# Moving a row gather, the weight casts of the first and last group, and the seam's small copies in a fused attention and mixer block

## The chip, the cores and the metric

The kernel runs as one launch on one NeuronCore of a Trainium2 chip. The metric is the device time of one execution in microseconds. The core has five engines with a queue each, and every queue runs in order: TensorE (PE; its weight loads are listed as PEld), VectorE (DVE), ScalarE (ACT), GpSimd (POOL) and SyncE (SP). SP and POOL issue the DMAs; POOL's are used where a transfer adds to what lies at its target.

## The reference

Everything is fp32, with x of 2048 rows (tokens) by 576 columns:

```python
xn  = layernorm(x)
out = x + A(xn) + B(xn)
# A: 32 heads of 18 columns; a token attends to itself and to 7 earlier tokens, 2 rows apart
q, k, v = split(xn @ wqkv);  A = softmax(q.k/sqrt(18), 8 taps) . v  @ wo
# B: spatial shift, then channel mixing
h  = gelu(layernorm(xn) @ w1)          # 576 x 576
hs = shift4(h, +1, -1, +2, -2) @ w2    # a quarter of the columns each, 576 x 576
x1 = xn + hs
B  = x1 + gelu(layernorm(x1) @ w3) @ w4   # 576 x 4608 and 4608 x 576
```

## The kernel before, in words

**Products in three parts.** A number is split into a high part that TensorE's fast fp32 format holds and the low rest. A product is then high by high, high by low and low by high. "Casting" an operand is always the same pair: ACT writes the high part (a copy or activation into the fp32r tile), and DVE subtracts it from the raw value and writes the low part. A raw operand comes by DMA, so the pair waits for its landing, and as ACT's queue runs in order, a cast that waits holds up whatever ACT has behind it: above all the copies that empty TensorE's PSUM banks.

**Stages, in order of time.** (1) q, k, v products (line 215 and 314), written to memory. (2) First mixing stage, lines 507 to 529: for each of 4 blocks `b` of 512 tokens, four tiles of W1's columns and one tile of remainders (`mix_rem`, line 478, PE line 482), in a fixed order; the block's input `xt` is read back by `get` (line 172) and cast by `split_x` (line 177). `mix_rem` also sends eight small transfers `v<-u` on SP. In the block `b == 1` SP also gathers tail rows of w3 from memory to memory into `w3t` (line 521), in two transfers, to be used much later. (3) Second mixing stage, line 628: 16 tiles `t` of 128 tokens (PE line 215), each with statistics on DVE and POOL; `n_turn` (582) normalises and transposes on ACT and DVE, and SP writes the turned blocks `xn` and reads them back (`get_n`). (4) Six plain pairs of W3's columns, line 1006: `up` (828, PE line 832) and `down` (859, PE line 868). (5) The rest of W3, 24 groups `q` (line 1192), twelve for each half `sb` of the tokens. Group 12 (`NWP`) is the first of the second half: around it lies the seam, where all seven token operands are loaded and cast anew (`get_op` 911, `split_op` 921). (6) The last eight `down` tiles (line 1391) and the product with Wo (1412 on).

**A group of stage 5.** It has seven products of half size (P1 to P7, Strassen's scheme, PE line 1127) and eight `down` tiles of the group before (D0 to D7, PE line 868). Their order on PE is written out in `ORDER`:

```
    ORDER = "P1 D0 P2 P6 D1 P5 D2 P7 D3 P4 D4 P3 D5 D6 D7"
    ORDERS = {0: "P1 P2 D0 P6 P5 P7 D1 D2 P4 D3 P3",
              NWP - 1: "P1 D0 P2 P6 P5 P7 D1 P4 P3 D2 D3 D4 D5 D6 D7",
              NWP: "D0 D1 P1 D2 P2 P6 D3 P5 P7 D4 P4 P3 D5 D6 D7"}
```

Behind each step the code issues that step's own work (emptying the bank: line 873 or 876 on ACT, 879 on DVE; seeding the next bank: 849; `keep`, ACT line 1133, saves a partial sum before PE adds to it; `z_add`, DVE line 1137; the gelus, ACT lines 814 to 821, and their low parts, DVE line 826), and then what `at(step, ...)` has planned there:

- `split_a(q)` casts W3's columns for the next group's products P1, P2 and P4 (A11, A12, A22). Step 0 is ACT line 967, step 1 is ACT line 969 on the tail rows and a POOL transfer that adds `w3t` (line 980), step 2 is DVE line 973. It waits for the pair's raw rows (`load_pair`, SP lines 951 and 954).
- `combine(q)` makes the sums of quarters in place (four DVE operations, line 962), and `split_s(q)` casts these for P3, P5, P6 and P7 (ACT 967 and 969, POOL 989, DVE 973).
- `split_w4` casts W4's rows (ACT 573, DVE 576), `split_wo(k)` one of Wo's five row blocks (ACT 200, DVE 201), which `load_wo` (line 1163) fetches at the start of the last group. In the last groups `o_turn`, `load_o` and `put_o` also turn and move the attention's output.

`split_op` works on one token operand: part 0 is ACT line 927 and DVE line 601 on the 256 main rows; part 1 is ACT line 932 (32 rows of the tail into a spare tile `r`), ACT line 933, and DVE line 601 on the tail.

**Attention** is a generator (`attention`, line 684) that fills DVE's time from stage 4 to group 18. For each of 8 groups of heads it multiplies q with k (line 746) and reduces (749) for 8 taps `w`, in singles and in doubles of two taps, and then weighs v (722, 726). `bg` lets it run for as long as a count of planned DVE time (`spent`) leaves over.

## Time and profile before

| | |
|---|---|
| time, median of 3 runs | 1281.77 us (1280.82 to 1283.99) |
| the profiled execution: its own time, its span | 1281.23 us, 1279.4 us |
| busy: PE, PEld, DVE, ACT, POOL | 98%, 90%, 70%, 57%, 20% of the span |
| TensorE's granted clock | 1.0 throughout |
| mean DMA rate | 174 GB/s |
| PE by stage 4's and 5's lines | L868 486.4 us, L1127 300.5 us, L832 157.0 us |

A row of a timeline has the start, the duration, the engine, the line, the operation and its tiles, and how often it is repeated; in brackets stands the idle time of the engine before it and what ended that. A row of waits has who waited and for whom, then the sum in us, how often, and the longest. `PE ps L868` is PE's instruction on tile `ps` at line 868; `SPq` is SP's queue, whose rows are DMA issues and not transfers.

### The profile page before, as it was taken

Reading aid. Unit: us, or ns where it says so; the run is one execution under the profiler, and the core shown is the slowest. Engines: PE = TensorE matmul, PEld = TensorE weight load, DVE = VectorE, ACT = ScalarE, POOL = GpSimd, SP = SyncE. Lnnn points to the kernel's source line nnn. Section 1 sums busy time; section 2 is a strip of 40 time slices with the busy share of each in tenths; the row PEclk is TensorE's granted clock in tenths of the full one; section 3 lists DMA queues with packets and bytes.
Section 4 is the critical chain, followed back from the end, with each engine's and each line's share of the span. In section 5 each row is a group of like instructions: output and inputs, shape, how many; then the busy total and the mean of one; then the engine's idle time right before and its main releaser. Section 6 shows DMA issues by size and latency. Waiting matters only on the chain.

```text
span 1279.4 us, 19983 instructions
## 1 busy us (share of the span) xinstructions
PE 1259.2 (98%) x7510; PEld 1154.4 (90%) x7510; DVE 897.7 (70%) x1196; ACT 727.3 (57%) x1162; POOL 252.8 (20%) x366
## 2 busy tenths in 40 slices
PE   8999999999999999999999999999999999999999
PEld 8999998799889998999889998998889999888898
DVE  6455534677648999998659998989798983554341
ACT  3332125525645545455777777776867776676630
POOL 2011100011122121212123232232121222222200
PEclk9999999999999999999999999999999999999999
DMA  7646784326887987769669988888958668899982
GB/s 207 154 122 140 166 173 144 103 87 196 209 237 166 223 149 164 150 141 242 120 143 205 199 173 214 201 174 223 259 92 184 124 110 192 178 211 216 256 247 84
DMA packets 203801, 223.25 MB, mean 174 GB/s; under 512 B 79528, under 2 KB 139528, under 8 KB 203576
## 3 DMA queue, kind: packets, MB, share of 16 engines
q1 hardware_dynamic: 170952, 155.18, 42.9%
q0 software_dynamic: 32752, 66.80, 32.1%
q8 instruction: 59, 0.97, 0.3%
q14 instruction: 38, 0.31, 0.1%
HBM read 124.47 MB, written 107.87 MB: 182 GB/s over the span
## 4 chain that ended last, share of the span: by engine, by line
PE 58%; DMA 6%; issue 3%; ACT 2%; DVE 1%; SPq 1%; POOL 0%; ACTq 0%; POOLq 0%; DVEq 0%
PE ps L868 27%; PE cc L1127 17%; PE p L832 9%; PE ps L215 4%; DMA w3st<-in_B_w_dram 2%; DMA xt<-td1T 1%; DMA v<-qkvd 1%; DMA td0T<-xn 1%; DMA x1n<-xd 1%; DVE L L749 0%; DMA x1n<-xn 0%; DMA w3s<-w3st 0%; DVE po L746 0%; SPq L1163 0%; PE p L1436 0%
## 5 line engine op out<-in xcount | busy, mean ns | idle before, releaser
L868 PEld LDWEIGHTS ps<-w,c 128*128 128x128 f32 x3456 | 475.3, 188 | 21.4 <-ACT Y L873 4.1
L868 PE MATMUL ps<-w,c 128*128 128x288 f32 x3456 | 486.4, 294 | 5.3 <-ACT Y L873 2.8
L874 POOL DMA_DIRECT2D yd<-Y x154 | 139.5, 909 | 389.8 <-ACT Y L873 317.4
L826 DVE TENSOR_TENSOR c<-Y,c 128x512 fp32r<-128x512 f32 x144 | 98.7, 687 | 89.5 <-ACT Y L815 87.0
L873 ACT COPY Y<-ps 128x576 f32<-128x576 f32 x154 | 98.0, 637 | 75.3 <-PE ps L868 66.3
L215 PE MATMUL ps<-WQ,xt 128*128 128x432 f32 x672 | 134.8, 360 | 0.0
L215 PEld LDWEIGHTS ps<-WQ,xt 128*128 128x128 f32 x672 | 125.6, 188 | 5.7
L1127 PE MATMUL cc<-xt,w3s 128*128 128x512 f32 (+1 forms) x504 | 127.8, 393 | 0.0
L1127 PEld LDWEIGHTS cc<-xt,w3s 128*128 128x128 f32 (+1 forms) x504 | 92.3, 188 | 17.8
L1127 PE MATMUL cc<-x1n,w3a 128*128 128x512 f32 (+1 forms) x336 | 86.4, 395 | 2.4 <-DMA w3a<-w3t 1.0
L746 DVE TENSOR_TENSOR po<-q,k 128x1152 f32<-128x1152 f32 (+1 forms) x48 | 84.2, 1754 | 1.0 <-DMA k<-qkvd 0.2
L749 DVE TENSOR_REDUCE L<-po 128x64 f32<-128x1152 f32 (+1 forms) x48 | 84.0, 1750 | 0.8
L876 ACT COPY Y<-ps 128x576 f32<-128x576 f32 x92 | 58.9, 640 | 41.7 <-PE ps L868 39.8
L122 POOL TENSOR_TENSOR rs<-rs,mhalf 128x1 f32<-128x1 f32 x48 | 30.9, 644 | 261.1 <-DVE rs L121 147.8
L324 ACT COPY stg<-ps 128x864 f32<-128x864 f32 x24 | 21.2, 882 | 102.8 <-PE ps L215 60.4
L814 ACT ACTIVATE c<-p 128x512 fp32r<-128x512 f32 x48 | 28.7, 599 | 85.7 <-PE p L832 85.7
L722 DVE TENSOR_TENSOR po<-v,L 128x1152 f32<-128x1152 f32 x56 | 75.4, 1353 | 0.8
L1127 PEld LDWEIGHTS cc<-x1n,w3a 128*128 128x128 f32 (+1 forms) x336 | 60.4, 188 | 14.5 <-ACT Y L821 1.4
L726 DVE TENSOR_TENSOR po<-po 128x1152 f32<-128x1152 f32 x49 | 66.4, 1354 | 0.9
L849 ACT COPY ps<-Y 128x576 f32<-128x576 f32 x92 | 59.4, 645 | 3.5 <-DVE Y L879 1.5
L1137 DVE TENSOR_TENSOR Y<-cc,Y 128x512 f32<-128x512 f32 x49 | 33.7, 688 | 35.2 <-ACT Y L1133 23.4
L215 PE MATMUL ps<-W,h 128*128 128x288 f32 x384 | 53.5, 295 | 0.0
(190 smaller groups left out, 1954.0 us busy)
## 6 DMA issues: line engine op xcount, KB each, us to landing
yd<-Y POOLq DMA_DIRECT2D x156, 288.0 KB, 6.1
Y<-in_B_w_dram SPq DMA_DIRECT2D x29, 576.0 KB, 6.5
w3st<-in_B_w_dram SPq DMA_DIRECT2D x56, 256.0 KB, 7.9
qkvd<-stg SPq DMA_DIRECT2D x24, 432.0 KB, 3.5
yd<-ev POOLq DMA_DIRECT2D x26, 288.0 KB, 6.8
w3st<-in_B_w_dram SPq DMA_DIRECT2D x92, 64.0 KB, 7.8
xd<-st SPq DMA_DIRECT2D x16, 320.0 KB, 5.9
xd<-big SPq DMA_DIRECT2D x16, 320.0 KB, 6.4
```

The costliest lines, as they stand in the source:

```text
L215: pe.matmul(ps[:, h, :n], xs(a), ws(b, h), start=i == 0, stop=i == len(PAIRS) - 1)
L722: dve.tensor_tensor(dst, vv, Lf[:, :, w:w + 1].to_broadcast([128, TPP * GH, HD]), op=ALU.mult)
L726: dve.tensor_tensor(o, o, dst, op=ALU.add)
L746: dve.tensor_tensor(dst, qf[:, None, :].to_broadcast([128, n, TPP * GC]), win, op=ALU.mult)
L749: dve.tensor_reduce(Lw[:, w:w + n, :], dst.rearrange("p w (x d) -> p w x d", d=HD), axis=AX.X, op=ALU.add)
L826: dve.tensor_tensor(h[:, 1, :], g, h[:, 0, :].bitcast(F32), op=ALU.subtract)
L832: pe.matmul(ps, W3[f][:, w, :], x1n[b][:, a, :], start=n == 0, stop=n == len(PAIRS) - 1)
L849: act.copy(ps[:, :, :HF], halves(t))
L868: pe.matmul(ps[:, k, :HF], h[:, col], w[:, p, k * HF:(k + 1) * HF], start=n == 0 and not seed, stop=n == len(seq) - 1, skip_group_check=True)
L873: act.copy(e.rearrange("p (h c) -> p h c", h=2), ps[:, :, :HF])
L874: pool.dma_start(yd[t], e, accum_op=ALU.add)
L1127: pe.matmul(ps, WX[w][:k, v, SLOT[w], :], area[sb][xk][:k, a, :], start=onto is None and i == 0, stop=last and i == len(HALVES) - 1, skip_ ...
```

## The change

Six edits in one:

1. The two gathers into `w3t` leave block `b == 1` of the first mixing stage and are issued behind tiles `t = 4` and `t = 5` of the second.
2. Attention's taps are grouped as singles 0 to 3 and doubles (4,5) and (6,7), where they were singles 0, 1, 2 and 7 and doubles (3,4) and (5,6).
3. In the second half of the tokens (`sb == 1`) the 32-row tail copy of `split_op` is a DVE `tensor_scalar` and no longer ACT line 932.
4. First group: `split_a` moves from D2 and P4 to P7 and D1, `combine` from P3 to P4. Seam group (`NWP`): `split_a` moves from P2 and P6 to P5 and P7, `combine` from D4 to P7, `split_s` from P3 and D5 to D5 and D6, `load_pair` from D6 to D7.
5. All other groups: `split_a` steps 0 and 1 move from D1 to P5 (groups 1 to 10) or to D2 (groups 13 to 22), and step 2 from D2 to P7 in groups 13 to 22.
6. Last group: `split_wo` 0 to 4 move from D5, D6, D7 and two of the eight last tiles to D1, P5, D2, P7 and D4.

```diff
@@ first mixing stage
-            if b == 1 and i in (2, 3):
-                r0, c0, n = ((256, 128, 128), (HF + 256, 0, 256))[i - 2]
-                sp.dma_start(w3t[:, :, 128 * (i - 2):128 * (i - 2) + n],
-                             dram_ap(w3, r0 * F + 256 * NPL + c0, [[256, NWP], [F, 32], [1, n]]))
@@ second mixing stage
+        if t in (4, 5):
+            r0, c0, n = ((256, 128, 128), (HF + 256, 0, 256))[t - 4]
+            sp.dma_start(w3t[:, :, 128 * (t - 4):128 * (t - 4) + n],
+                         dram_ap(w3, r0 * F + 256 * NPL + c0, [[256, NWP], [F, 32], [1, n]]))
@@ attention
-                for w, n in ((0, 1), (1, 1), (2, 1), (3, 2), (5, 2), (7, 1)):
+                for w, n in ((0, 1), (1, 1), (2, 1), (3, 1), (4, 2), (6, 2)):
@@ split_op
-            act.activation(r[64:96], raw[64:96, 0, :], AF.Identity, scale=sg)
+            if sb:
+                dve.tensor_scalar(r[64:96], raw[64:96, 0, :], sg, None, op0=ALU.mult)
+            else:
+                act.activation(r[64:96], raw[64:96, 0, :], AF.Identity, scale=sg)
@@ first group, q == 0
             at("P6", split_op, 0, "T4")
             at("D1", gelu22)
+            at("P7", split_a, n, (0, 1))
             at("D1", split_op, 0, "B22")
+            at("D1", split_a, n, (2,))
             at("D2", low22)
-            at("D2", split_a, n, (0, 1))
-            at("P4", split_a, n, (2,))
+            at("P4", combine, n)
             at("P3", gelu12)
-            at("P3", combine, n)
+            at("P3", split_s, n, (0, 1))
             at("P3", low12)
-            at("P3", split_s, n, (0, 1))
             at("P3", split_s, n, (2,))
@@ seam group, q == NWP
-            at("P2", split_a, n, (0, 1))
-            at("P6", split_a, n, (2,))
             at("P6", split_op, 1, "T4", 1)
             at("D3", split_op, 1, "B22", 0)
             at("P5", split_op, 1, "B22", 1)
-            at("D4", combine, n)
+            at("P5", split_a, n, (0, 1))
+            at("P7", split_a, n, (2,))
+            at("P7", combine, n)
             at("D4", gelu22)
-            at("D6", load_pair, q + 2)
             at("P4", low22)
-            at("P3", split_s, n, (0, 1))
             at("D5", gelu12)
-            at("D5", split_s, n, (2,))
+            at("D5", split_s, n, (0, 1))
             at("D6", low12)
+            at("D6", split_s, n, (2,))
+            at("D7", load_pair, q + 2)
@@ other groups
-            at("D1", split_a, n, (0, 1))
-            at("D2", split_a, n, (2,))
+            at("P5" if q < NWP else "D2", split_a, n, (0, 1))
+            at("D2" if q < NWP else "P7", split_a, n, (2,))
@@ last group
-            for k, it in enumerate(("D5", "D6", "D7")):
+            for k, it in enumerate(("D1", "P5", "D2", "P7", "D4")):
                 at(it, split_wo, k)
@@ last eight tiles
-        if j in (1, 4):
-            split_wo(3 + j // 3)
```

## The prediction

> **What bounds the kernel now.** I read the page first, then PE's waits stretch by stretch, then the queue of the engine that each wait names.

> ```profile
> span 1279.4 us, 19983 instructions
> PE 1259.2 (98%) x7510; PEld 1154.4 (90%) x7510; DVE 897.7 (70%) x1196; ACT 727.3 (57%) x1162; POOL 252.8 (20%) x366
> ```

> PE is busy for all but 20 us, and no edit takes work from PE. So a gain can only come out of those 20 us, a few tenths to a microsecond at a time, and an edit that keeps ACT or DVE waiting can open new gaps of any length. Each part below takes PE's gaps in its stretch as what can be won, and replays ACT's and DVE's queues in the new order.

> **Groups 13 to 22, the cast one product on.** PE's waits between 1080 and 1170 us, and ACT's queue at the first of them:

> ```profile
> PE cc L1127 <- ACT Y L1133: 2.2, 3, 0.8
> ```

> ```profile
> 1090.26 0.83 ACT L967 CAST w3a<-w3st 128x768 fp32r<-128x768 f32 x1 [3.38 <-DMA w3st<-in_B_w_dram]
> 1091.00 0.61 ACT L969 ACTIVATE w3a<-w3st,kv 96x384 fp32r<-96x384 f32 x1
> 1091.52 0.62 ACT L876 COPY Y<-ps 128x576 f32<-128x576 f32 x1
> 1092.17 0.64 ACT L849 COPY ps<-Y 128x576 f32<-128x576 f32 x1
> 1092.75 0.58 ACT L1133 COPY Y<-cc 128x512 f32<-128x512 f32 x1
> ```

> P4 waits three times for P7's `keep` (L1133), because `split_a` stood idle on its raw rows for 3.4 us with D2's emptying and seed (L876, L849) behind it, and `keep` behind those. With `split_a` behind D2, the two copies run inside that idle time. `keep` can come earlier by at most their spacing, 1.23 us (1091.52 to 1092.75), and by nothing if D2 ended only as the rows landed. I take 0.65 us, which leaves little of a stall of 0.7: **-1.9 us** of 2.2, with ends -2.2 and 0. POOL's `w3t` addition and the subtraction move with the cast; their reader, the next group's P1, is seven steps off. `combine` now stands behind that subtraction (0.9 us) and ahead of nothing that PE waits for in this group.

> In groups 1 to 10 the move from D1 to P5 changes no queue: P5 puts nothing on ACT, so the cast stays between the copies of D1 and D2. Nothing. Attention's new grouping has the same operations; a double stands later by one single, and its cover is that PE does not name attention in any wait: nothing, within 0.5 us to either side.

> **The seam.** PE's waits between 890 and 940 us, the tail copy that moves (a row by form of 880 to 935 us), its nearest DVE relative, and ACT's late cast:

> ```profile
> PE ps L868 <- ACT Y L873: 1.9, 2, 1.3
> PE cc L1127 <- ACT Y L1133: 1.3, 2, 1.1
> ```

> ```profile
> L932 ACT ACTIVATE Y<-xt 32x512 fp32r<-32x512 f32 x4 | 2.5, 628 | 0.1
> ```

> ```profile
> L498 DVE TENSOR_SCALAR u<-u,low 128x512 f32<-128x512 f32 x4 | 1.9, 482 | 1.4 <-ACT u L494 1.4
> ```

> ```profile
> 929.73 1.05 ACT L967 CAST w3s<-w3st 128x1024 fp32r<-128x1024 f32 x1 [2.93 <-DVE w3st L962]
> ```

> Seven tail copies of 0.63 us leave ACT, which is what is late here: 4.4 us less in its queue. That covers the first wait for L873 (0.6 us, one such copy ahead of it) and the waits for P7's `keep`. The longest wait, 1.3 us before D7, is for D5's emptying, which stands behind `split_s` (L967 above, 1.05 us, and its tail, after 2.9 us of waiting for `combine`). With `combine` two steps earlier and `split_s` behind D5's emptying it goes. What is late next is D6's emptying and the next group's seed, now behind `split_s`: I leave 0.4 us there. So **-2.8 us** of 3.2. The DVE copies are not in the trace; the tail's form with two tensors is dearer, the 128-row scalar form costs 0.48, and I take that, 7 x 0.48 = 3.4 us on a DVE that mostly waits for ACT here. Ends: -3.2, and +3.4 if every copy fell on the path and nothing was won. `load_pair` one step on still waits for the same `split_s` transfer on SP; nothing.

> **The gather.** PE's waits between 230 and 250 us, SP's queue, ACT's wait for the block, and the DMA share behind the gather's new place (columns: stretch, its length, busy time of PE, PEld, DVE, ACT, POOL, clock, DMA share, GB/s):

> ```profile
> PE ps L482 <- DVE xt L188: 0.9, 1, 0.9
> PE ps L482 <- ACT g L473: 0.9, 1, 0.9
> PE ps L482 <- ACT xt L187: 0.2, 1, 0.2
> ```

> ```profile
> 229.72 0.85 SPq L521 DMA_DIRECT2D w3t<-in_B_w_dram  x1
> 230.68 1.80 SPq L174 DMA_DIRECT2D xt<-xd  x2
> ```

> ```profile
> ACT xt L181 <- DMA xt<-xd: 3.2, 2, 2.2
> ```

> ```profile
> 284.00:290.00 6.00, 6.00 (x47) 6.00 (x47) 3.13 (x11) 0.00 (x0) 1.48 (x4) 1.00 0.93 182
> ```

> The last block's read stands behind both gathers on SP, so it is issued some 1.9 us earlier without them (twice 0.85 and the gaps), and its packets no longer queue behind the second gather's. ACT's 2.2 us wait for it goes, and with it the waits for L473 and L187. The lows (L188) come 2.2 us earlier, but PE asks for them 1.1 us earlier, so I leave 0.3 us of the 0.9. That is -1.8 us. In the second stage SP is free at t = 4; at t = 5 the wider gather goes ahead of the turned block's writes and W4's read, on a DMA that is busy to 0.93 just behind it. ACT's casts of W4 and of the first blocks wait behind these. I take 0.3 us that reaches PE: **-1.5 us**, with ends -2.1 and, if ACT's 2.2 us wait reappears there less what the gather gains in DVE's pauses, +0.5.

> **The first group.** PE's waits between 630 and 650 us, DVE's queue and ACT's:

> ```profile
> PE cc L1127 <- DMA w3a<-w3t: 1.0, 1, 1.0
> PE cc L1127 <- ACT w3a L967: 0.6, 1, 0.6
> PE cc L1127 <- DVE w3a L973: 0.5, 1, 0.5
> PE cc L1127 <- ACT cc L1330: 0.3, 1, 0.3
> ```

> ```profile
> 632.42 1.23 DVE L601 SCALAR_TENSOR_TENSOR xt<-xt 128x1024 fp32r<-128x1024 f32 x1 [1.78 <-ACT xt L927]
> 633.68 0.68 DVE L601 SCALAR_TENSOR_TENSOR xt<-xt,Y 32x512 fp32r<-32x512 f32 x1
> 634.39 0.76 DVE L879 TENSOR_TENSOR Y<-ps,Y 128x576 f32<-128x576 f32 x1
> 635.07 0.68 DVE L826 TENSOR_TENSOR c<-Y,c 128x512 fp32r<-128x512 f32 x1
> 636.62 0.96 DVE L973 TENSOR_TENSOR w3a<-w3st,w3a 128x768 fp32r<-128x768 f32 x1 [0.87 <-ACT w3a L967]
> 637.50 0.68 DVE L1137 TENSOR_TENSOR Y<-cc,Y 128x512 f32<-128x512 f32 x1
> 638.10 2.32 DVE L962 TENSOR_TENSOR w3st<-w3st 128x384 f32<-128x384 f32 x4
> ```

> ```profile
> 638.88 0.63 ACT L821 ACTIVATE Y<-Y 128x512 f32<-128x512 f32 x1
> 640.50 1.05 ACT L967 CAST w3s<-w3st 128x1024 fp32r<-128x1024 f32 x1 [0.99 <-PE cc L1127]
> ```

> The cast of group 1's weights at P7 removes the first three waits, 2.1 us. But two things come late in their place. ACT now does `split_a` (1.4 us, part of it in a pause of 0.3) ahead of B22's cast, so DVE's first row starts about 1.05 us later, at 633.5. And `combine` (2.3 us) now stands at P4, ahead of P3's `z_add` (L1137). All seven rows run without a pause: 7.3 us, so `z_add` ends at 640.8, where it ended at 638.2. Behind it ACT does the two gelu passes (0.6 each) and only then the cast L967, which starts at 642.0 instead of 640.5. Its tail and L1330's copy follow, and PE's P2 waits for that copy (the fourth row). So P2, where both orders meet, comes 1.5 us later: **+1.5 us**. Ends: -2.4 if DVE is not in the way, +2.5 if the raw rows land 1 us after ACT asks for them.

> **The last group.** PE's waits from 1195 us to the end; SP's fetch of Wo, the time to landing of line 1163, and P4 on PE:

> ```profile
> PE ps L868 <- ACT ps L849: 1.0, 2, 0.5
> PE ps L868 <- ACT Y L873: 0.9, 1, 0.9
> ```

> ```profile
> 1185.88 4.72 SPq L1163 DMA_DIRECT2D wr<-in_A_wo_dram  x4
> ```

> ```profile
> DMA to landing us min/median/max: 6.7/7.3/7.5
> ```

> ```profile
> 1191.65 1.78 PE L1127 MATMUL cc<-xt,w3a 128*128 128x512 f32 x7
> ```

> Taking three casts from D5 to D7 and two from the last tiles frees ACT where PE waits 1.9 us; I count 1.5, since the 0.9 stands behind `split_x` as well. But the first cast now stands at D1, the second at P5, the third at D2, all ahead of P7's `keep`, for which P4 waits. Wo's blocks are issued from 1185.88 on, about 1.5 us apart, and take 7: they land near 1192.8, 1194.8 and 1196.2. A cast has the size of the seed's copy above (L849, 0.64). ACT stands still until the second block: 1194.8 + 0.64, then D2's emptying and seed (1.23), the third cast (0.64) and `keep` (0.58): 1197.9. P4 started at 1191.65 and would start at 1198.0, 6.4 us later, and everything behind it. Net **+4.9 us**. Ends: -1.9 if the blocks were there in time, +6.9 if the tail keeps its waits and the restart costs a little. The cover that the old places had was the 15 us from issue to first use.

> **Sum.** -1.9 - 2.8 - 1.5 + 1.5 + 4.9 = +0.2 us on the profiled execution's own 1281.23 (its span of 1279.4 and 1.8 us around it), so 1281.4; the median of the runs lies 0.54 above that execution, which gives **1282.0**.

> **The rivals.** (1) *Slower: the wait for Wo swallows what was won before it.* If the landing is set by a crowded DMA queue and not by PE's progress, what groups 18 to 21 win is only waited out (+1.9), the tail's waits return behind the delayed group (+1.5), and half the seam's gain goes to DVE (+1.4): 1286.8. For it: the landing of 7 us for 288 KB. Against it: the fetch is issued from the same program position, which moves with PE. It decides from a landing later than 1192.5.

> (2) *Faster: Wo lands soon enough.* The quickest transfer of this size on SP:

> ```profile
> yd<-Y SPq DMA_DIRECT2D x8, 288.0 KB, 2.6
> ```

> At 2.6 us the third block lands near 1191.8, `keep` ends at 1193.1, P4 loses 1.4 and the tail wins 1.9: the last group is then -0.4 instead of +4.9, in all 1276.7. Against it: the three rows of landings above, all near 7.

> (3) *The seam's copies cost what they save.* POOL's issues are held by DVE in places without sharing data:

> ```profile
> POOL yd L874 <- DVE w3st L962: 14.1, 5, 3.7
> ```

> Seven copies of 0.48 us ahead of POOL's additions could delay the buffers that ACT's copies need, and the seam gives +0.5 instead of -2.8: 1285.3. [...]

> (4) *The first group wins after all*, -2.4 instead of +1.5, if `combine` finds a pause in DVE: 1278.1.

> **How the numbers follow.** The likeliest case, gains and losses that cancel, has 0.40 (its own range 1279 to 1285), rival 1 0.25, rival 2 0.15, rivals 3 and 4 0.10 each. About 0.3% (3.8 us) is what a measurement of this kernel tells from no change: 1277.9 to 1285.6. Faster: rival 2, half of rival 4 and a little of the likeliest, 0.22. Slower: rival 1, half of rival 3 and a little of the likeliest, 0.33. The same: 0.45. The range from 1276.5 to 1287.3 reaches over both outer rivals and leaves out less than 2 in 10.

> **What would show it.** Right: no PE wait at L482; PE waits for L1133 in groups 18 to 21 and in the seam near zero; P2 of group 1 late behind L967; in the last group ACT L200 idle for several us on `wr`, and one PE wait of 6 us for L1133. Wrong: no such wait at L200 (then rival 2), POOL waiting for DVE in the seam (rival 3), or a new PE wait in the second mixing stage, which I count at 0.3.

## The result, and the profile after

The changed kernel takes 1287.01 us (median of 7 runs, 1284.88 to 1290.09) where the kernel before takes 1282.60 (7 runs, the three of the table above among them): a ratio of 1.0036, with a 95% interval of 1.0024 to 1.0049. It is slower by 4.4 us. The profiled execution took 1286.14 us; span and clock of it, and its engines:

```profile
core 0: 1284.3 us, clock 0.994
span 1284.3 us, 19963 instructions
PE 1263.6 (98%) x7510; PEld 1158.5 (90%) x7510; DVE 900.2 (70%) x1203; ACT 721.2 (56%) x1155; POOL 252.8 (20%) x366
```

PE's work is the same, yet its busy time grew by 4.4 us, and the granted clock, 1.000 before, averages 0.994. Both belong together, as the last group shows below.

Where the time went can be read from PE alone: its matmuls are the same ones in the same order, so each can be found in both traces, and the difference of the two starts is what the change has won (-) or lost (+) up to there. Lines of the changed file are numbered 3 higher from about L930 on (product is L1130, keep L1136, z_add L1140) and 4 lower between the moved gather's two places (L597 was L601).

| stretch, up to PE's matmul | start before | start after | offset | this stretch | forecast |
|---|---|---|---|---|---|
| first mixing stage | 246.25 | 243.37 | -2.88 | -2.9 | -1.8 |
| second mixing stage and first units | 334.99 | 331.64 | -3.35 | -0.5 | +0.3 |
| first group, to P2 of group 1 | 642.71 | 641.13 | -1.58 | +1.8 | +1.5 |
| groups up to the seam | 823.28 | 821.45 | -1.82 | -0.2 | 0 |
| seam | 935.28 | 932.36 | -2.92 | -1.1 | -2.8 |
| groups 13 to 22 | 1167.49 | 1164.16 | -3.33 | -0.4 | -1.9 |
| last group, P4 starts | 1191.65 | 1195.04 | +3.39 | +6.7 | +6.4 |
| matmuls behind it | 1194.86 | 1201.07 | +6.21 | +2.8 | 0 |
| last tiles | 1210.64 | 1215.54 | +4.90 | -1.3 | -1.5 |

**The last group.** ACT's queue in the changed kernel (the bracket is the idle time before the row and what ended it), and PE's:

```profile
1191.41 1.28 ACT L200 CAST Wo<-wr 128x576 fp32r<-128x576 f32 x2 [8.69 <-DMA wr<-in_A_wo_dram]
1192.60 0.63 ACT L876 COPY Y<-ps 128x576 f32<-128x576 f32 x1
1193.26 0.64 ACT L849 COPY ps<-Y 128x576 f32<-128x576 f32 x1
1193.84 0.67 ACT L200 CAST Wo<-wr 128x576 fp32r<-128x576 f32 x1
1194.41 0.58 ACT L1136 COPY Y<-cc 128x512 f32<-128x512 f32 x1
```

```profile
1186.71 1.75 PE L868 MATMUL ps<-w,c 128*128 128x288 f32 x12
1195.04 3.35 PE L1130 MATMUL cc<-xt,w3a 128*128 128x512 f32 x7 [6.58 <-ACT Y L1136]
1198.19 3.08 PE L868 MATMUL ps<-w,c 128*128 128x288 f32 x12
```

ACT stands 8.7 us in front of a cast of Wo whose rows have not landed; keep (L1136), for which P4 waits, is the fifth instruction behind. Then comes what no row of before could show: P4's seven matmuls take 3.35 us, where the same seven took 1.78 before, and the twelve of D4 3.08 instead of 1.75. The stretches of 1 us, with the granted clock as the third figure behind the stretch (its length, PE's busy time and count, the clock, DMA share, GB/s):

```profile
1190.00:1191.00 1.00, 0.00 (x0) 0.99 1.08 351
1191.00:1192.00 1.00, 0.00 (x0) 0.50 1.06 348
...
1200.00:1201.00 1.00, 1.00 (x6) 0.50 1.09 341
1201.00:1202.00 1.00, 1.00 (x6) 0.89 1.14 240
```

The clock falls to half at 1190.97, 2.5 us after PE's last matmul (it ended at 1188.46), so PE restarts at half clock, and it comes back at 1201.21, 6.2 us after the restart.

**The first group.** DVE's queue, and PE's row at D0 of group 1:

```profile
634.00 2.33 DVE L965 TENSOR_TENSOR w3st<-w3st 128x384 f32<-128x384 f32 x4
636.25 0.68 DVE L1140 TENSOR_TENSOR Y<-cc,Y 128x512 f32<-128x512 f32 x1
```

```profile
637.65 1.04 PE L868 MATMUL ps<-w,c 128*128 128x288 f32 x4 [3.11 <-ACT c L820]
```

```profile
638.00:639.00 1.00, 0.69 (x4) 0.51 0.79 145
639.00:640.00 1.00, 0.96 (x4) 0.50 0.08 16
```

combine (L965) runs ahead of z_add (L1140), gelu of c12 (L820) waits for z_add, and D0, which reads c12, waits 3.1 us. Behind that gap the clock is at half again, from 638.01 to 641.43 us. The three waits for group 1's weights are gone.

**The seam.** PE's waits from 890 to 940 us, and DVE's queue where the longest begins:

```profile
PE cc L1130 <- DVE Y L1140: 1.0, 1, 1.0
PE ps L868 <- DVE Y L879: 0.4, 1, 0.4
PE ps L868 <- ACT Y L873: 0.3, 1, 0.3
PE ps L868 <- ACT ps L849: 0.2, 1, 0.2
```

```profile
918.11 1.36 DVE L746 TENSOR_TENSOR po<-q,k 128x1152 f32<-128x1152 f32 x1
919.39 1.22 DVE L597 SCALAR_TENSOR_TENSOR xt<-xt 128x1024 fp32r<-128x1024 f32 x1
920.53 0.68 DVE L826 TENSOR_TENSOR c<-Y,c 128x512 fp32r<-128x512 f32 x1
921.24 0.42 DVE L933 TENSOR_SCALAR Y<-xt 32x512 fp32r<-32x512 f32 x1
921.70 0.68 DVE L597 SCALAR_TENSOR_TENSOR xt<-xt,Y 32x512 fp32r<-32x512 f32 x1
922.41 0.69 DVE L1140 TENSOR_TENSOR Y<-cc,Y 128x512 f32<-128x512 f32 x1
```

ACT is hardly late any more (L873 and L849, 0.5 us). DVE has not a single pause here; z_add, whose data ACT had ready at 919.7 (keep, 919.12 and 0.59), starts at 922.41. A piece of attention (L746) stands in this queue as well as the copies (L933, 0.42 us each).

**Groups 13 to 22.** No wait of PE is listed between 940 and 1170 us. But ACT's rows in a group that had no stall before, P4's start in that group and the next, and the same two of before:

```profile
1065.10 0.83 ACT L970 CAST w3a<-w3st 128x768 fp32r<-128x768 f32 x1
1065.83 0.61 ACT L972 ACTIVATE w3a<-w3st,kv 96x384 fp32r<-96x384 f32 x1
1066.35 0.56 ACT L1136 COPY Y<-cc 128x512 f32<-128x512 f32 x1
```

```profile
1066.96 1.86 PE L1130 MATMUL cc<-xt,w3a 128*128 128x512 f32 x7
...
1091.27 1.86 PE L1130 MATMUL cc<-xt,w3a 128*128 128x512 f32 x7
```

```profile
1044.35 1.79 PE L1127 MATMUL cc<-xt,w3a 128*128 128x512 f32 x7
...
1068.41 1.79 PE L1127 MATMUL cc<-xt,w3a 128*128 128x512 f32 x7
```

A group takes 24.31 us now (1091.27 - 1066.96) and took 24.06 (1068.41 - 1044.35). keep runs directly behind the cast, and P4 starts a little late in every group: ten times 0.24 us, 2.4 us, against 2.7 us that the three stalls of before had cost. The list of waits does not show these delays; only the distance from start to start does.

### The profile page after: what moved, and what is told of

The parts are those of the page before. It is cut to its first block, busy times and chain, and to the rows that moved or that the text cites. A ratio compares the mean times of both kernels' runs of the same rounds, so it can differ in the third digit from the quotient of the medians.

```text
span 1284.3 us, 19963 instructions
## 1 busy us (share of the span) xinstructions
PE 1263.6 (98%) x7510; PEld 1158.5 (90%) x7510; DVE 900.2 (70%) x1203; ACT 721.2 (56%) x1155; POOL 252.8 (20%) x366
## 4 chain that ended last, share of the span: by engine, by line
PE 60%; DMA 4%; ACT 3%; DVE 2%; issue 1%; SPq 1%; DVEq 0%; ACTq 0%; POOLq 0%
PE ps L868 29%; PE cc L1130 17%; PE p L832 10%; PE ps L215 4%; DMA w3st<-in_B_w_dram 1%; DMA x1n<-xn 1%; DMA xt<-xn 1%; DMA wr<-in_A_wo_dram 1%; DMA xt<-td1T 0%; SPq L169 0%; DMA x1n<-td1T 0%; DVE xt L597 0%; DVE w3st L965 0%; SPq L1178 0%; ACT Y L873 0%
## 5 line engine op out<-in xcount | busy, mean ns | idle before, releaser
L868 PEld LDWEIGHTS ps<-w,c 128*128 128x128 f32 x3456 | 477.5, 189 | 23.0 <-ACT c L820 3.5
L868 PE MATMUL ps<-w,c 128*128 128x288 f32 x3456 | 488.8, 295 | 6.3 <-ACT c L820 3.1
L874 POOL DMA_DIRECT2D yd<-Y x154 | 139.3, 908 | 388.2 <-ACT Y L873 330.9
L826 DVE TENSOR_TENSOR c<-Y,c 128x512 fp32r<-128x512 f32 x144 | 98.8, 687 | 93.0 <-ACT Y L815 88.0
L873 ACT COPY Y<-ps 128x576 f32<-128x576 f32 x154 | 97.9, 636 | 74.7 <-PE ps L868 62.0
L1130 PE MATMUL cc<-xt,w3s 128*128 128x512 f32 (+1 forms) x504 | 128.0, 394 | 1.0 <-DVE Y L1140 1.0
L1130 PEld LDWEIGHTS cc<-xt,w3s 128*128 128x128 f32 (+1 forms) x504 | 92.3, 188 | 19.2 <-DVE Y L1140 1.4
L876 ACT COPY Y<-ps 128x576 f32<-128x576 f32 x92 | 58.9, 640 | 65.7 <-PE ps L868 64.3
L1130 PE MATMUL cc<-x1n,w3a 128*128 128x512 f32 (+1 forms) x336 | 86.1, 395 | 0.1
L746 DVE TENSOR_TENSOR po<-q,k 128x1152 f32<-128x1152 f32 (+1 forms) x48 | 84.2, 1755 | 0.8
L1140 DVE TENSOR_TENSOR Y<-cc,Y 128x512 f32<-128x512 f32 x49 | 33.7, 687 | 53.5 <-ACT Y L1136 48.7
L1130 PEld LDWEIGHTS cc<-x1n,w3a 128*128 128x128 f32 (+1 forms) x336 | 60.7, 189 | 11.4 <-DVE w3a L976 0.4
L849 ACT COPY ps<-Y 128x576 f32<-128x576 f32 x92 | 59.4, 646 | 4.4 <-DVE Y L879 2.4
## 6 DMA issues: line engine op xcount, KB each, us to landing
yd<-Y POOLq DMA_DIRECT2D x156, 288.0 KB, 6.0
yd<-ev POOLq DMA_DIRECT2D x26, 288.0 KB, 7.1
```

Source lines behind the costliest of these rows:

```text
L746: dve.tensor_tensor(dst, qf[:, None, :].to_broadcast([128, n, TPP * GC]), win, op=ALU.mult)
L826: dve.tensor_tensor(h[:, 1, :], g, h[:, 0, :].bitcast(F32), op=ALU.subtract)
L849: act.copy(ps[:, :, :HF], halves(t))
L868: pe.matmul(ps[:, k, :HF], h[:, col], w[:, p, k * HF:(k + 1) * HF], start=n == 0 and not seed, stop=n == len(seq) - 1, skip_group_check=True)
L873: act.copy(e.rearrange("p (h c) -> p h c", h=2), ps[:, :, :HF])
L874: pool.dma_start(yd[t], e, accum_op=ALU.add)
```

## The experiments

The theory after this reading: six independent terms, the sizes of the table, with the last group's wait and the lowered clock behind it as the one that turns the sum. The parts with a forecast were undone or done alone; attention's new grouping (edit 2, forecast at nothing) has no run of its own. "Before" is the kernel before on the chip of that run (medians 1281.77, 1282.46, 1282.19 and 1282.16 in the four sets). Differences in us are those of the medians; the ratios are not always the quotients of these medians (c9: 0.9931, the medians give 0.9920).

**c1, the casts of Wo back in their old places.**

```
-            for k, it in enumerate(("D1", "P5", "D2", "P7", "D4")):
+            for k, it in enumerate(("D5", "D6", "D7")):
...
+        if j in (1, 4):
+            split_wo(3 + j // 3)
```

> The changed kernel with the casts of Wo back in their old places (D5, D6, D7 of the last group and two of the last tiles). Theory: the last group alone makes the change slower, by a wait for Wo's rows (6.7 us) and by matmuls at half clock behind it (2.8 us), less 1.3 us won in the tail. Then PE has no wait of microseconds before P4 of the last group, the granted clock stays at 1.0 there, and the time falls by 8.2 us against the changed kernel: a median near 1278.8. Rival: the waits of the seam and the 0.24 us in each of groups 13 to 22 carry the loss, and the last group only shows it late; then it falls by 5 us or less, to 1282 or above.

Measured: 1279.17 us, 0.998 of before (0.9972 to 0.9989). The rest of the change is a gain, and the last group alone turns it into a loss: it costs 7.0 us by the differences to before (+4.4 and -2.6) and 7.8 us from median to median (1287.01 - 1279.17, from different sets of runs). In the two profiles PE's starts shift by 8.3 us between the last matmuls ahead of P4 and the end, as the theory had it.

**c2, the kernel before with that one edit.**

> The kernel before with only the casts of Wo moved as in the change. Theory: the wait is set by the fetch, which is issued from the same place of the program and moves with PE; so it costs the same 8.2 us as in the changed kernel: a median near 1290.8. Rival: the landing is set by the DMA queues and not by PE, and 3.3 us of the wait were there only because PE came 3.3 us earlier; then it costs 4.9 us: a median near 1287.5.

Measured: 1289.03 us, 1.0062 (1.0047 to 1.0077), +7.3 us. PE waits as long as in the changed kernel, although it does not come early here:

```profile
PE cc L1127 <- ACT Y L1133: 6.8, 1, 6.8
```

SP issues the fetch at 1186.47 here, 2.7 us later than in the changed kernel (1183.81), where PE is 2.9 us earlier. So the fetch moves with PE, as was argued against rival 1. The total is between the two expectations because the clock came back sooner, by 1201 us, 3 us after P4's start at 1198.14: the matmuls lost 1.4 us (offset +6.49 at P4's start, +7.89 at the last of its seven), not 2.8, and the tail won the same 1.4 us back.

**c3, the first group's plan alone.**

> The kernel before with only the first group's plan of the change. Theory: the three waits for group 1's weights go (2.5 us), and D0 of group 1 waits 3.3 us for the gelu pass that stands behind z_add, which stands behind combine; the granted clock then falls to 0.5 for some 3 us and costs 1.1 us: +1.8 us in all, a median near 1284.4. Rival: the wait at D0 is as long in the changed kernel only because PE came 3.3 us earlier there; then it shrinks, the clock stays at 1.0, and the plan wins up to 2.4 us: near 1280.2.

Measured: 1284.80 us, 1.0028 (1.0017 to 1.0038), +3.0 us. The profile shows the same two waits as the changed kernel, 3.1 us for L820 and 0.5 for L826, and a loss of 1.8 us in this group, the theory's figure. The wait does not need the gather's head start. The mean clock of the eleven runs is 0.996 to 0.999. The profiled execution is the quickest of the eleven; where the others lose the 1.2 us more is not shown.

**c4, the gather alone.**

> The kernel before with only the gather moved to the second mixing stage. Theory, from the changed kernel's trace: PE's three waits in the first mixing stage go whole (2.9 us) and 0.5 us of the wait at 335 us goes as well: -3.35 us, a median near 1279.2. Rival, as forecast: 0.3 us is lost in the second stage and the lows still cost 0.9 us: -1.5 us, near 1281.1.

Measured: 1278.46 us, 0.9983 (0.9974 to 0.9991), -3.3 us. Yet its profiled execution took 1281.16, and three others of its twelve runs lie between 1280 and 1281.3 as well; the rest lie between 1277.2 and 1279.2. In the profiled one PE waits twice behind the second mixing stage (at 322 and 347 us), and ACT waits 1.5 us longer for a turned block's read than in the changed kernel's profile. PE's waits and ACT's row in c4, and then ACT's row in the changed kernel:

```profile
PE p L832 <- ACT Y L815: 1.3, 1, 1.3
PE ps L868 <- ACT Y L873: 1.2, 1, 1.2
```

```profile
317.42 0.63 ACT L606 ACTIVATE xt<-xt 64x512 fp32r<-64x512 f32 x1 [3.80 <-DMA xt<-xn]
```

```profile
314.45 0.63 ACT L606 ACTIVATE xt<-xt 64x512 fp32r<-64x512 f32 x1 [2.32 <-DMA xt<-xn]
```

What the first stage wins is given back in such executions: PE comes early, the read does not. It is issued 1.7 us earlier than in the kernel before (309.40 against 311.07), yet ACT gets its rows at 317.42, where it got them at 317.55. PE's offset to before goes from -2.34 us behind the first stage to -0.17 at 350 us. These waits stand in the profiles of c1, c8 and c11 as well and not in those of the changed kernel, c10 and c12, all with the gather in the same place; what decides between the two stays open.

**c5, the seam alone.** The new plan of group 12 and the copies on VectorE, on the kernel before.

> The kernel before with the seam's part of the change alone (the new plan of the group at the seam, and its tail copies on VectorE). Theory, from the changed kernel's trace: ACT is no longer late, but the copies, 0.42 us each, fill VectorE's queue, so that z_add and the sums of the down tiles come late and PE waits for them (1.1, 0.6, 0.4 us): a net of -1.1 us, a median near 1280.7. Rival, as forecast: VectorE has room and the seam wins 2.8 us, near 1279.0, the waits in the changed kernel coming from what stood before the seam.

Measured: 1280.73 us, 0.9982 (0.9971 to 0.9993), -1.7 us; in the profiles the seam itself gives -1.2, with the changed kernel's waits for L1140 and L879, 1.0 and 0.4 us, and one of 0.7 us for the copy at L1333 that the changed kernel does not have.

**c6, the same with the copies left on ACT.**

> The same without the copies: the seam's new plan, the tail copies still on ACT. Theory (VectorE's queue is the new bound): PE's wait for z_add goes, but ACT is late again and PE waits for P7's keep as before; the plan alone wins the 1.5 us before D7 and loses some of it at D6: -1.0 us, near 1280.8, the same as with the copies moved. Rival: ACT's 4.4 us were the whole matter; then the plan alone wins nothing or loses up to 1.5 us: 1281.8 to 1283.3.

Measured: 1281.44 us, 0.9987 (0.9974 to 1.0000). PE waits for ACT again:

```profile
PE cc L1127 <- ACT Y L1133: 1.5, 1, 1.5
PE cc L1127 <- ACT cc L1330: 0.9, 1, 0.9
PE ps L868 <- ACT Y L873: 0.6, 1, 0.6
```

Moving the copies is worth 0.7 us by the medians, which the intervals do not separate, and as much by the profiles (the seam gives -0.45 us here, -1.2 in c5): it trades ACT's lateness for DVE's.

**c7, the cast of groups 13 to 22 alone.**

> The kernel before with only the cast of groups 13 to 22 (and 1 to 10) one product on. Theory: P7's keep now stands behind the cast in every group, and P4 starts 0.24 us later in each of ten groups, which gives back 2.4 of the 2.7 us of the three waits that go: -0.3 us, near 1281.5. Rival: the 0.24 us come from another part of the change; then -2.2 us, near 1279.6.

Measured: 1281.52 us, 0.9991 (0.9979 to 1.0003). No difference that can be told; in its profile the delays of 0.24 us are there and the three stalls are not. The five parts that were run alone (c2, c3, c4, c5, c7) add up to +4.4 us by their medians, the change's own difference, which leaves nothing for attention's grouping; each has an interval of 1 us or more to either side, so that it comes out so evenly is luck.

**c8, the changed kernel mended.** Beside c1's edit:

```
-            at("P5" if q < NWP else "D2", split_a, n, (0, 1))
-            at("D2" if q < NWP else "P7", split_a, n, (2,))
+            at("D1" if q < NWP else "P7", split_a, n, (0, 1))
+            at("D2" if q < NWP else "D3", split_a, n, (2,))
...
-            at("P7", split_a, n, (0, 1))
+            at("P7", split_a, n, (0, 1, 2))
+            at("P7", combine, n)
...
-            at("D1", split_a, n, (2,))
-            at("P4", combine, n)
...
-            at("P3", split_s, n, (0, 1))
             at("P3", low12)
+            at("P3", split_s, n, (0, 1))
```

> The changed kernel mended by what its trace shows: the casts of Wo in their old places; in groups 13 to 22 the cast behind P7's keep and z_add instead of ahead of it; in the first group combine already behind the cast at P7, and the low part of c12 ahead of the next cast, so that z_add finds VectorE free. Theory: 8.2 us from the last group, 2.4 us from ten groups, 3.6 us from the first group (no wait of 3 us at D0, the clock stays at 1.0) against the changed kernel: a median near 1272.8. Rival: the cast behind P7 only moves the late rows' wait to D3's emptying, and B22, half a microsecond later, holds P3 of the first group: then only the last group's part and half of the first group's come, near 1277.

Measured: 1273.97 us, 0.9934 (0.9918 to 0.9949): 12.9 us under the changed kernel by the differences to before (-8.5 and +4.4). ACT now runs keep first and the cast behind it,

```profile
1087.30 0.59 ACT L1136 COPY Y<-cc 128x512 f32<-128x512 f32 x1 [0.25 <-PE cc L1130]
1087.78 0.84 ACT L970 CAST w3a<-w3st 128x768 fp32r<-128x768 f32 x1
```

groups 13 to 22 have neither stalls nor delays (offset to the kernel before -4.26 behind the seam, -6.62 in group 21: -2.4 us), and the first group wins 1.5 us on before (offset -0.64 to -2.16) instead of losing 1.8.

**c9, three more edits on c8.** The first three casts of Wo at P3; `spent[0] += 1.15 if sb else 0.7` for a tail part; the gather in units 2 and 3.

> The mended kernel (c8) with three more edits, each in a stretch of its own. (1) The last group's first three casts of Wo at P3 instead of D5, D6, D7, where ACT stood idle for 2.6 us and the rows had landed: theory, PE's waits of 0.53 and 0.46 us for L849 go, -1.0 us; rival, the rows land too late for P3 and D5's emptying waits. (2) The planner is told what a tail copy costs VectorE in the seam (1.15 us for the part instead of 0.7), so that attention's pieces stay out of the seam: theory, PE's wait of 0.97 us for z_add goes, -1.0 us; rival, the z_add is late by the tails themselves and nothing changes. (3) The gather behind the mixing stages, in the second and third of the units that follow: theory, the waits of 1.2 and 1.4 us at 321 and 347 us stay in the profile, as the block's read is slow for another reason, 0; rival, the gather slows that read, then -2.8 us where these waits were. In all 1272.0 by the theories, 1269.2 with the last rival.

Measured: 1271.90 us, 0.9931 (0.9915 to 0.9946), the lowest of all, though its interval and c8's overlap; what each edit gives is read from the two profiles alone. Against c8's profile the last tiles win 1.0 us (offset -4.12 to -5.11): the waits for L849 go, 1.2 us, and 0.2 us of it are lost at the wait that is left (L869 here, 1.1 us; L873 in the other files, 0.9 us). The seam wins 1.2 us (offset -2.55 ahead of it, -3.75 at the down tile where c8 waits for L879): the waits for L1140 and L879 are gone once the planner knows what the copies cost, though a new one of 0.7 us for L869 comes in at 902 us. The waits at 321 and 347 us are gone, but they are also absent in the profile of c10, which has the gather where c8 has it. So edit (3) is not shown to be what removed them, and neither its theory nor its rival is settled; what makes the read slow stays open.

**c10, a longer gap in the first group.** `for _ in range(3): at("D3", low22)` on c8.

> The mended kernel (c8) with three low parts computed again on VectorE ahead of P3's z_add in the first group (the same values written again), so that PE's gap before D0 of group 1 grows from 0.34 to about 2.2 us. Theory: it takes a gap near 3 us to lower the granted clock, so the clock stays at 1.00 and the time grows by the gap alone, +1.9 us on c8: near 1275.9. Rival: any gap well above the 1.3 us seen without effect lowers it; then about 1.1 us more, near 1277.

Measured: 1283.01 us, 1.0001 (0.9988 to 1.0014): neither. The gap is 2.5 us and does lower the clock, so the theory falls there; and much more is lost in waits far from the edit (at 763, 877 and 962 us, with the clock lowered twice more, behind the first two; some 7 us against c12 below, which has the same gap). PE's waits from 640 to 980 us:

```profile
PE cc L1130 <- DMA w3a<-w3t: 2.9, 1, 2.9
PE ps L868 <- ACT Y L873: 2.1, 2, 1.6
PE cc L1130 <- ACT Y L1136: 2.0, 2, 1.8
```

**c11 and c12, two and three repeats, not told to the planner** (`spent[0] -= 0.69` behind each).

> The mended kernel (c8) with two low parts computed again on VectorE ahead of z_add in the first group, the same values written again, and this time not told to the planner, so that attention's pieces stay where c8 has them. PE's gap before D0 of group 1 is then about 1.9 us (0.34 and twice 0.61 and what the third brought in c10). Theory: the clock falls after gaps of 2.5 us and more alone; it stays at 1.00 here, and the time is c8 and 1.3 us, near 1275.3. Rival: it falls at 1.9 us as well, 0.8 us more.

> The same with three, as in c10 but not told to the planner. Theory: the gap is 2.5 us again and the clock falls to 0.5 for about 3 us behind it (+2.2 and +0.8 us), while the waits of c10 at 763, 877 and 962 us are gone, since they came from attention's pieces, which the planner had put 2 us later: near 1277.0. Rival: those waits come from the gap itself, which shifts PE against the transfers; then they stay and the time is that of c10, 1283.

Measured: c11 1274.82 us, 0.9952 (0.9938 to 0.9965); c12 1276.08, 0.9960 (0.9945 to 0.9975); both within a microsecond of the theory. In c12 the distant waits of c10 are gone: c10 and c12 differ only in the 2.1 us of VectorE time that the planner was told of and by which it placed attention's pieces, so these waits come from there. How the moved pieces hold up POOL's addition to w3a stays open. c11's profile, one of its slower executions, has two distant waits of its own, though the planner was not told (for L1136, 2.2 us together, at 774 and 799 us). The clock in c11 (gap of 1.78 us from 637.55) and in c12 (gap of 2.51 us):

```profile
639.00:640.00 1.00, 0.67 (x4) 1.00 1.28 92
```

```profile
640.00:641.00 1.00, 1.00 (x5) 0.50 0.06 16
```

c11's profile bears the theory out, its other runs do not quite: the mean clock is below 1.000 in five of its nine runs, in three of c12's four, and in two of twelve of the kernel before on that chip. Only the profiled executions show where the clock fell, so it is not shown that this gap lowered it in the others. Why a gap of one length lowers it at one time and not at another stays open; the last section has the gaps that the profiles show.

## Why the prediction was right in its range and wrong in its sum, step by step

1282.0 was forecast with the likeliest case that gains and losses cancel; 1287.0 was measured. That is inside the range, 0.3 us from its upper end, but above the likeliest case's own 1279 to 1285 and above the 1285.6 from which it counts as slower, which had a chance of 0.33 against 0.45 for the same. The range held because it reached over rival 1, whose reasons did not come true, so that it held is in part luck. The step that failed by most is the last group's term.

- *Last group, +4.9, measured +8.2* (c2 alone +7.3, c1 undone -8). The mechanism was right in each step: ACT idle at L200, one PE wait for keep, a wait that moved P4 by 6.7 us where 6.4 were counted, 1.3 us won back in the tail where 1.5 were counted. The term left out what PE does after the wait: it restarted at half clock, 2.8 us. "The restart costs a little" stood only in the upper end, with 0.5 us.
- *Gather, -1.5, measured -3.35* (c4 -3.3). All three waits went, the lows' (L188) too, of which 0.3 us had been left standing. The cost in the second stage, +0.3, was absent in the changed kernel's profile (-0.5) and near +2.2 in c4's, where 0.2 us of the gain is left at 350 us; four of the seven profiles with the gather in this place have such waits. The case stood in the forecast as the upper end of +0.5.
- *Seam, -2.8, measured -1.1* (c5 -1.2 in the trace). ACT's lateness went as said, and a copy on VectorE cost 0.42, near the 0.48 taken. What failed is the cover, "a DVE that mostly waits for ACT": in before DVE was busy for 23.2 of the 30 us from 905 to 935, and what pauses it had, ACT's lateness made. With ACT in time it is busy for 26.3 us of that stretch (902 to 932 in the changed kernel), and from 912.6 to past z_add without a pause. Rival 3 had the copies cost what they save, but through POOL. POOL does wait once for DVE in the seam (7.3 us, L826), the sign named for it, but no wait of PE there names POOL, and PE's two longest waits there are for VectorE's own queue (L1140 and L879).
- *Groups 13 to 22, -1.9, measured -0.4* (c7). The three stalls went. Missed: the forecast counted keep's gain in the three groups with late rows and not its loss in every group, where the cast, 1.35 us, now ran just ahead of keep; the order behind keep costs nothing (c8).
- *First group, +1.5, measured +1.8* (c3 +3.0 by the medians). combine ahead of z_add was the cause, as said. The place was not P2, which waits for the copy of cc, but D0 before it, which reads c12. Of the 1.8 us 1.1 are the lowered clock, which the forecast did not have; without it the group would have lost 0.7, so the match of +1.5 and +1.8 is luck.
- *Rival 1* gave 1286.8, by luck and not for its reasons: the wait did not swallow earlier gains (c2 waits as long without them), and the tail's waits did not return. Only its loss in the seam was there. Rivals 2 and 4 fall with the rows of ACT's wait and of D0's.

The two terms that were too hopeful (seam and groups, 3.2 us together) and the clock (2.8 us) outweigh the gather's larger gain (1.8 us).

## What to carry to other kernels

Put work that may wait for a transfer behind the copy that TensorE waits for next, never ahead of it: the cast of W3 cost 0.24 us in each group ahead of keep and nothing behind it, and the cast of Wo ahead of keep, with its rows still in flight, cost 6.7 us. When an engine is relieved, count the idle time of the engine that takes the work over as it will be, not as it was while it waited for the first; and tell the planner of the work that is moved (c9), but read the profile again afterwards, as what it moves in turn can cost more (c10). Count a gap on TensorE as possibly longer than it is: behind one of 1.83 us (c10) and behind those of 2.5 to 6.8 us half the granted clock for 3 to 6 us of matmuls came on top here, 0.8 to 2.8 us of lost time, and none behind one of 1.82 us (c6).

## What had not been expected of the hardware

```profile
876.54 2.83 PE L1130 MATMUL cc<-xt,w3a 128*128 128x512 f32 x7 [1.83 <-ACT Y L1136]
878.00:879.00 1.00, 1.00 (x4) 0.50 1.03 234
```

```profile
335.80 1.85 PE L868 MATMUL ps<-w,c 128*128 128x288 f32 x12 [1.82 <-ACT ev L873]
337.00:338.00 1.00, 1.00 (x8) 1.00 0.08 16
```

One of 1.78 us left it at 1.00 in c11 as well. The two gaps above differ by 0.01 us; what decides between them is not shown, as no run placed one gap at several times. What lets the clock rise again stays open too: it came back 6.2 us after PE's restart in the changed kernel (6.58 us of gap) and 3 us after it in c2 (6.8 us).
